# Where the gate products stand in a tile, and when the second group of scores is taken, in a fused attention and feed-forward kernel

## The chip, the cores and the metric

The kernel runs on one core of one Trainium2 chip. The metric is the device time of one launch in microseconds (us), lower is better. Engines: PE multiplies matrices, DVE, ACT and POOL work on tiles element by element, SP issues DMAs. Each engine takes its instructions in program order, and the order of the program is written out by hand.

## The reference

Linear attention with projected keys and values, then a gated feed-forward block on the result:

```python
k_proj = einsum('ks,bhsd->bhkd', E, k); v_proj = einsum('ks,bhsd->bhkd', F, v)   # B=H=8, S=1024, D=64, 64 rows
attn   = softmax(q @ k_proj^T / sqrt(D))                                          # over the 64 projected keys
x      = (attn @ v_proj) as [8192, 512]
g      = x @ w_gate                                                               # [8192, 1536]
out    = ((g * sigmoid(g)) * (x @ w_val)) @ w_out                                 # float32 [8192, 512]
```

## The kernel before, in words

The 8192 tokens are cut into 16 chunks `c` of 512 tokens, two to a batch `b`. The feed-forward block of a chunk runs in 12 tiles `f` of 128 gate columns, so there are 192 tiles, `t = 12c + f`. While the two chunks of batch b-1 run, the attention of batch b is worked in between them: `put(s, fn, ...)` puts a step into a slot, and tile t has slot 2t (between its gate and value products on PE) and slot 2t+1 (at its end). Slot numbers in `place(b)` count from the first tile of the even chunk of that stretch, so slot 23 is the end of tile 11 of the even chunk, and slot 25 the end of tile 0 of the odd one.

A tile runs in this order: `f_g` (gate matmuls, L536 into a `gps` bank, then Silu on ACT, L563), slot 2t, `f_v` (value matmuls, L536 into a `vps` bank), the list `late[t]`, slot 2t+1. There are two `gps` banks and two `vps` banks.

**Gate products.** A plain tile ends with one DVE product, L678: Silu of the gate times the value, read from its `vps` bank, written to `hT` in bf16. From chunk 4 on (in part from chunk 3) the tiles 2-3, 5-6 and 8-9 are paired: the value products of a pair are made with seven half-size products (L616) instead of eight, spread over three tiles. Tile p (2, 5 or 8) runs `p_34` in place of the value matmuls, and later in its `late` list `p_1`, which writes the other `vps` bank. Tile p+1 runs `p_52`, and tile p+2 (4, 7 or 10, itself plain) runs `p_76` before its value matmuls. `p_52` and `p_76` each end with a DVE sum L627, which empties the `vps` bank into `sx`, and a DVE product L634 of `thp` and `sx`, both in SBUF. `p_34` has the ACT copy L644, the Silu L646, which frees the `gps` bank of tile p, and the DVE sum L647.

**Output products.** The product with `w_out` of chunk c-1 runs during chunk c, also with seven half-size products, twice (for two halves of the tokens): `f_m(c, n)` takes them in the order 3, 4, 5, 2, 1, 6, 7. Products 1 and 6 stand together in `late` of tile 4 (first half) and tile 10 (second half), product 7 in tile 5 and tile 11. Called m1 to m7 here, each is 6 matmuls, L762. After m6 stands `m_16`: the DVE addition L791, which reads the bank that m1 wrote and that m7 will add to, and then the POOL subtraction L792. After m7 stands `m_7`: the DVE addition L797, which empties the bank and needs L792.

The operands of m1, m2, m5, m6 and m7 are sums of parts of `hT` (`h_sum`, L745). Those for m5 and m2 are made on POOL in tiles 7 to 11, one `f` at a time. Those for m1, m6 and m7 are made on DVE, each by one instruction, in tiles 1, 2 and 4 of the next chunk. The one for m7, here h7, is appended to `late` of tile 4 behind m1, m6 and L791, one tile ahead of m7. The operands that the paired tiles need of x are made by four DVE sums L607 (`p_x`), for an odd chunk all in tile 0.

**Attention steps.** `u_KV` projects keys and values, `u_KT` turns the keys and copies them into `BD` by two ACT and two DVE copies, one after another (L299 on DVE). `u_S` makes scores (L378) and takes Exp on ACT (L386), `u_R` sums and inverts on DVE (L408, L409), `u_N` normalises on POOL (L423, then a small L439), `u_AD` turns the result by a DMA that SP issues. A batch has eight `u_S`, j = 0 to 7, in two groups of four. Exp and Tanh share one function table of ACT, Silu is in another, and a change of table is an instruction of its own (ACT_TABLE_LOAD). So that the table changes twice for a group and not four times, the tile whose Silu falls between two pairs of scores is made with Tanh (the list `TANGENT`): Tanh on ACT, L560, and two DVE instructions, L681 and L684, in place of L678.

Of the kernel before, what the change touches and what calls it, by code (L numbers as in the profile page):

```python
# [10 lines left out]
ALU = mybir.AluOpType  # L11
# [4 lines left out]
B = 8  # L16
# [17 lines left out]
HT = CW // 2  # L34
ENG = [getattr(mybir.EngineType, n) for n in ("PE", "DVE", "Activation", "SP", "Pool")]
TANGENT = [(c, f) for c in range(CH) for f in range(NFT)] + [
    x for b in range(2, B) for x in ((2 * b - 2, 8 if b == 2 else 7), (2 * b - 1, 1))
]
PAIRED = {2: range(4, NC), 5: range(3, NC), 8: range(3, NC - 1)}
BY_DMA = [(b, ch) for b in range(1, B) for ch in range(CH)]  # L40
# [3 lines left out]
def kernel(  # L44
# [19 lines left out]
    nc = tc.nc  # L64
# [38 lines left out]
    kb, vb, qb, xT, hT = {}, {}, {}, {}, {}  # L103
# [421 lines left out]
    def f_mm(c, f, w, i=None):  # L525

        if i != 1:


            where = "y" if (c, f, w) == (0, 2, 0) else "gv"[w]  # L530
            half[c, f, w] = bank(where, [P, CW], FP32, where + "ps")
        ps = half[c, f, w]
        x = xT[divmod(c, CH)]
        ts = slice(0, CW) if i is None else slice(256 * i, 256 * (i + 1))
        for kt in range(NKT):
            nc.tensor.matmul(  # L536
                out=ps[:, ts],
                lhsT=(wg, wv)[w][:, kt, f * P : (f + 1) * P],
                rhs=x[:, kt, ts],
                start=(kt == 0),  # L540
                stop=(kt == NKT - 1),
            )
        return ps

    def paired(c, f):
        p = 3 * ((f + 1) // 3) - 1
        return p if not maxed and c in PAIRED.get(p, ()) and f < p + 2 else None

    def f_g(c, f, i=None):
        ps = f_mm(c, f, 0, i)  # L550
        p = paired(c, f)
        if p is not None:
            if f == p:
                gp["g"] = ps
            else:
                nc.scalar.activation(out=gp["p"][:, 1], in_=ps[:], func=AF.Silu)  # L556
            return
        th = fw.tile([P, CW], FP32, name="th", tag="th")
        if (c, f) in TANGENT and not maxed:
            nc.scalar.activation(out=th[:], in_=ps[:], func=AF.Tanh, scale=0.5)  # L560
            gp[0] = (ps, th)
        else:
            nc.scalar.activation(out=th[:], in_=ps[:], func=AF.Silu)  # L563
            gp[0] = (None, th)

    sums = {}

    def p_tiles():


        for n in range(2):
            a = q_pool.tile([P, 8, HT], BF16, name="xsa", tag=f"q0{n}", bufs=1)
            for m, x in ((6, a[:, 0:2]), (7, a[:, 2:4]), (67, a[:, 0:4]), (1, a[:, 4:6]), (3, a[:, 6:8])):
                sums["x", m, n] = x
        sums["x", 4, 0] = quarter(wo, 0, 1)[:, 4:6]
        sums["x", 4, 1] = x4[:]
        rows = [quarter(wo, 0, 1)[:, i] for i in range(4)] + [quarter(wo, 1, 0)[:, i] for i in range(HF)]
        for i, m in enumerate((1, 2, 5, 6, 7)):
            sums["w", m, 2] = wp[:, i]
            for n, f in enumerate((5, 8)):  # L580
                sums["w", m, f] = rows[5 * n + i].rearrange("p (k t) -> p k t", k=2)
# [47 lines left out]
    def p_h(c, p, part, v):  # L629
        h, th = (  # L630
            a.rearrange("p i t -> p (i t)").rearrange("p (i t) -> p i t", i=4)[:, part]
            for a in (hT[c][:, p : p + 2, :], gp["p"][:])
        )
        nc.vector.tensor_tensor(out=h, in0=th, in1=v, op=ALU.mult)  # L634

    def p_34(c, p):

# [16 lines left out]
    def p_52(c, p):  # L654
        x, sx = gp["x"], gp["sx"]
        p_mm(c, p, 5, x[:, 0])
        p_mm(c, p, 2, x[:, 1])
        p_sum(sx[:], gp["ts"][:, 0], x[:], ALU.subtract)
        p_h(c, p, slice(1, 3), sx[:])

    def p_76(c, p):
        x, sx = gp.pop("x"), gp.pop("sx")
        p_mm(c, p, 7, x[:, 0])
        p_mm(c, p, 6, x[:, 1])
        p_sum(sx[:], gp.pop("ts")[:, 1], x[:], ALU.add)
        p_h(c, p, slice(0, 4, 3), sx[:])
        gp.pop("p")

    def f_v(c, f, i=None):
        p = paired(c, f)  # L670
        if p is not None:
            return (p_34, p_52)[f - p](c, p)
        ps = f_mm(c, f, 1, i)
        g, th = gp.pop(0)
        if f == 0:
            hT[c] = h_pool.tile([P, NFT, CW], BF16, name="hT", tag="hT")
        if g is None:
            nc.vector.tensor_tensor(out=hT[c][:, f, :], in0=th[:], in1=ps[:], op=ALU.mult)  # L678
            return
        s1 = fw.tile([P, CW], FP32, name="s1", tag="s1", bufs=1)  # L680
        nc.vector.scalar_tensor_tensor(  # L681
            out=s1[:], in0=th[:], scalar=1.0, in1=g[:], op0=ALU.add, op1=ALU.mult
        )
        nc.vector.scalar_tensor_tensor(  # L684
            out=hT[c][:, f, :], in0=s1[:], scalar=0.5, in1=ps[:], op0=ALU.mult, op1=ALU.mult
        )
# [173 lines left out]
    def put(s, fn, *a):  # L860
        slots[s].append((fn, a))

    def place(b):
        s0 = 48 * (b - 1)
        if b == 1:
            put(22, u_TD, 1, 0)
            put(29, u_K1, 1)
            put(32, u_KT, 1)
            put(40, u_V1, 1)
            sa = (35, 36, 37, 38, 41, 42, 43, 44)  # L870
            put(41, u_AD, 1, 0)
            put(30, u_TD, 1, 1)
            put(47, u_AD, 1, 1)
            put(46, u_PVt, 1, 0, (0, 1), ("aa", "av"))
        else:
            if b == 2:
                put(s0 + 10, u_KV, b)
            else:
                put(s0 + 8, u_KV, b, "kv", (0, H), "v")
            put(s0 + (13 if b == 2 else 11), u_KT, b)  # L880
            put(s0 + (9 if b == 2 else -6), u_TD, b, 0)
            put(s0 + (11 if b == 2 else -4), u_TD, b, 1)
            sa = [s0 + j for j in ((15, 15, 17, 17) if b == 2 else (13, 13, 15, 15)) + (25, 25, 27, 27)]
            put(s0 + 29, u_AD, b, 0)
            put(s0 + 43, u_AD, b, 1)
            put(s0 + 44, u_PVt, b, 0, (0, 1), ("aa", "yz"))
        for j in range(NJ):
            put(sa[j], u_S, b, j)
            at = sa[j] + 1 if b == 1 else s0 + (
                17, 17 + 2 * (b == 2), 21 if b == 2 else 19, 23, 35, 37, 40, 41)[j]  # L890
            put(at, u_R, b, j)
            put(at, u_N, b, j)
        put(s0 + (68 if b == 1 else 56), u_PVt, b, 1, (0, 1), ("aa", "yz"))

    def run_slot(s):
        for fn, a in slots.pop(s, ()):
            fn(*a)
# [16 lines left out]
    def general():  # L914
# [6 lines left out]
        with tc.For_i(0, B) as turn, tc.manual_schedule():  # L921
            turn_of.append(turn)
            b = 0
            load_k(b)
            load_v(b)
            u_KV(b)
            u_KT(b)
            for ch in range(CH):
                c = CH * b + ch
                load_q(b, ch)  # L930
                for u in range(4 * ch, 4 * ch + 4):
                    u_T(b, u)
                    u_S(b, u)
                    u_R(b, u)
                    u_N(b, u)
                    u_A(b, u)
                u_PVt(b, ch, (0, 1), ("aa", "yz"))
                for f in range(NFT):
                    f_g(c, f)
                    f_v(c, f)  # L940
                for m in (1, 2, 5, 6, 7):
                    h_sum(c, m, 0, HF, nc.vector)
                for n in range(14):
                    f_m(c, n)

    with tc.manual_schedule():
# [3 lines left out]
        for i in range(2):  # L950
            nc.scalar.dma_start(
                out=kraw[i][:],
# [126 lines left out]
        for b in range(1, B):  # L1079
            place(b)  # L1080
        for b in range(2, B):
            s0 = 48 * (b - 1) - (20 if b == 3 else 24)
# [10 lines left out]
        late = defaultdict(list)  # L1093
# [25 lines left out]
        for c in range(3, NC):  # L1119
            for i, m in enumerate((4, 3, 1, 67)):  # L1120
                t = c * NFT + (0 if c % 2 else (-1, -1, 0, 0)[i])
# [7 lines left out]
        for t in range(NIT):  # L1129
            c, f = divmod(t, NFT)  # L1130
            ring["wide"] = c < 2
            i = 1 if t < 2 else None
            f_g(c, f, i)
            if "x" in gp and paired(c, f) is None:
                p_76(c, f - 2)
            run_slot(2 * t)
            f_v(c, f, i)
            for fn, *a in late.pop(t, ()):
                fn(*a)
            run_slot(2 * t + 1)  # L1140
        f_m_last(NC - 1)
# [33 lines left out]
```

## Time and profile before

| | us |
|---|---|
| median of 3 runs | 556.23 (556.15 to 557.1) |
| the profiled execution, its own time | 556.3 |
| its span, first to last instruction | 554.7 |
| PE busy | 532.3 (96%) |
| DVE busy | 436.0 (79%) |
| POOL busy | 343.9 (62%) |
| ACT busy | 293.5 (53%) |
| granted clock of PE | 1.000 |

From batch 3 on the trace repeats with a period of about 66.6 us, two chunks of 12 tiles. A row of the timeline holds the start, the time busy, the engine, the line, the operation, what is written and read with shapes, and in brackets how long the engine was idle ahead of it and which instruction ended that. The end of a matmul is modelled and lies some 0.16 us behind the time at which the next one can start, so the brackets of PE show that much too little; the time lost is read from the starts.

### The profile page before, as it was taken

How to read it: one execution, taken by the hardware profiler on the slowest of the kernel's cores; microseconds unless marked ns; L12 is line 12 of the kernel's file. 1: busy time of each engine (PE TensorE's matmuls, PEld its weight loads, DVE VectorE, ACT ScalarE, POOL GpSimd, SP SyncE). 2: the span in 40 equal slices, each digit the busy share in tenths (PEclk: the TensorE clock that was granted, in tenths of full speed). 3: DMA queues.
4: the chain of work that ended last, by engine and by line, in shares of the span. 5: the costliest groups of instructions: out<-in, count | busy, mean ns of one | idle time of the engine just before them, and what ended most of it. 6: DMA issues, size and time to landing. Idle time of an engine off the chain costs nothing. (4 is left out here: it accounts for less than half of the span.)

```text
span 554.7 us, 9971 instructions
## 1 busy us (share of the span) xinstructions
PE 532.3 (96%) x3712; PEld 334.4 (60%) x3780; DVE 436.0 (79%) x712; ACT 293.5 (53%) x527; POOL 343.9 (62%) x428
## 2 busy tenths in 40 slices
PE   7999999999999899999999999999999999999996
PEld 4654445566566565666666666565665666566665
DVE  3787885688878897789877887879887798875874
ACT  3564454674457644656546565565554844453431
POOL 7862494395925968178861878538683584835344
PEclk9999999999999999999999999999999999999999
DMA  9999969839901399105971179611993112200013
GB/s 199 191 197 189 176 143 181 161 78 193 224 1 39 86 201 207 40 2 122 209 163 39 41 113 212 132 39 40 155 204 99 39 52 63 77 37 16 26 40 116
DMA packets 112228, 62.94 MB, mean 113 GB/s; under 512 B 65968, under 2 KB 103856, under 8 KB 112176
## 3 DMA queue, kind: packets, MB, share of 16 engines
q0 software_dynamic: 43952, 29.49, 37.2%
q1 hardware_dynamic: 67392, 31.46, 22.6%
q10 hardware_dynamic: 832, 1.31, 0.8%
q8 instruction: 30, 0.49, 0.3%
q14 instruction: 22, 0.18, 0.1%
HBM read 60.29 MB, written 16.78 MB: 139 GB/s over the span
## 5 line engine op out<-in xcount | busy, mean ns | idle before, releaser
L536 PE MATMUL gps<-xT,wg 128*128 128x512 bf16 (+1 forms) x727 | 192.0, 377 | 5.0 <-ACT thp L646 3.3
L745 POOL TENSOR_TENSOR hs<-hT 128x256 bf16<-128x256 bf16 x180 | 133.7, 773 | 7.0 <-DVE hT L678 4.4
L536 PE MATMUL vps<-xT,wv 128*128 128x512 bf16 (+1 forms) x459 | 118.8, 376 | 1.4 <-DMA wv<-in_moe_w_val_dram 0.8
L536 PEld LDWEIGHTS <-wg 128*128 128x128 bf16 x776 | 74.0, 98 | 55.7 <-issue 4.7
L792 POOL TENSOR_TENSOR tt<-tt,ysb 128x512 f32<-128x512 f32 x28 | 43.7, 1560 | 101.0 <-DVE tt L791 98.9
L762 PEld LDWEIGHTS <-hs 128*128 128x128 bf16 x900 | 86.9, 98 | 31.6 <-issue 5.8
L563 ACT ACTIVATE th<-gps 128x512 f32<-128x512 f32 x82 | 49.0, 597 | 92.0 <-PE gps L536 87.2
L423 POOL TENSOR_TENSOR AAd<-ee,zr 128x512 bf16<-128x512 f32 x56 | 61.6, 1100 | 37.8 <-ACT ee L386 17.8
L536 PEld LDWEIGHTS <-wv 128*128 128x128 bf16 x480 | 45.1, 98 | 50.7 <-issue 6.5
L762 PE MATMUL yps<-ws,hs 128*128 128x256 bf16 x540 | 68.7, 273 | 6.0 <-DVE tt L791 3.8
L678 DVE TENSOR_TENSOR hT<-th,vps 128x512 bf16<-128x512 f32 x82 | 55.7, 679 | 23.0 <-PE vps L536 18.9
L634 DVE TENSOR_TENSOR hT<-thp,sx 128x512 bf16<-128x512 f32 x74 | 63.3, 856 | 6.4 <-ACT thp L556 1.8
L627 DVE TENSOR_TENSOR sx<-ts,vps 128x512 f32<-128x512 f32 x74 | 49.4, 667 | 12.2 <-PE vps L616 10.9
L781 POOL TENSOR_TENSOR tt<-xs 128x256 f32<-128x256 f32 x30 | 27.1, 905 | 46.5 <-ACT xs L779 46.5
L762 PE MATMUL yps<-ws,hT 128*128 128x256 bf16 x360 | 48.8, 273 | 0.6
L762 PE MATMUL yps<-wo,hs 128*128 128x256 bf16 x360 | 48.6, 273 | 0.1
L745 DVE TENSOR_TENSOR hs<-hT 128x1536 bf16<-128x1536 bf16 (+1 forms) x49 | 47.9, 985 | 0.0
L644 ACT COPY sx<-vps 128x512 f32<-128x512 f32 x37 | 21.7, 585 | 48.6 <-PE vps L616 48.0
L408 DVE TENSOR_REDUCE zr<-ee 128x8 f32<-128x512 f32 x64 | 42.9, 670 | 3.1 <-ACT ee L386 3.1
L762 PEld LDWEIGHTS <-hT 128*128 128x128 bf16 x360 | 35.2, 98 | 13.2
L386 ACT ACTIVATE ee<-sc 128x512 f32<-128x512 f32 x64 | 36.2, 602 | 9.6 <-POOL AAd L423 5.3
L647 DVE TENSOR_TENSOR ts<-sx 128x256 f32<-128x256 f32 x37 | 25.4, 688 | 16.8 <-ACT sx L644 16.8
(134 smaller groups left out, 741.5 us busy)
## 6 DMA issues: line engine op xcount, KB each, us to landing
out_dram<-ysb SPq DMA_DIRECT2D x27, 512.0 KB, 2.9
qb<-in_q_dram POOLq DMA_DIRECT2D x14, 512.0 KB, 18.0
kb<-in_k_dram POOLq DMA_DIRECT2D x7, 1024.0 KB, 10.4
vb<-in_v_dram POOLq DMA_DIRECT2D x7, 1024.0 KB, 16.6
wo<-in_moe_w_out_dram POOLq DMA_DIRECT2D x2, 768.0 KB, 21.7
out_dram<-ysb SPq DMA_DIRECT2D x6, 256.0 KB, 2.4
kraw<-in_k_dram ACTq DMA_DIRECT2D x2, 512.0 KB, 4.8
qb<-in_q_dram POOLq DMA_DIRECT2D x4, 256.0 KB, 7.9
```

The costliest lines, as they stand in the source:

```text
L386: nc.scalar.activation(out=e[:].rearrange("p h j k -> p (h j k)"), in_=ps[:].rearrange("p a k -> p (a k)"), func=AF.Exp, scale=scale,)
L408: nc.vector.reduce_sum(out=z, in_=e[:], axis=AX.X)
L423: eng.tensor_tensor(out=a.rearrange("p j h k -> p h j k"), in0=ee.pop((b, u))[:], in1=r.unsqueeze(3).to_broadcast([P, 4, 2, KP]), op=ALU.mult,
L536: nc.tensor.matmul(out=ps[:, ts], lhsT=(wg, wv)[w][:, kt, f * P : (f + 1) * P], rhs=x[:, kt, ts], start=(kt == 0), stop=(kt == NKT - 1),)
L563: nc.scalar.activation(out=th[:], in_=ps[:], func=AF.Silu)
L627: nc.vector.tensor_tensor(out=out, in0=a.unsqueeze(1).to_broadcast([P, 2, HT]), in1=b, op=op)
L634: nc.vector.tensor_tensor(out=h, in0=th, in1=v, op=ALU.mult)
L678: nc.vector.tensor_tensor(out=hT[c][:, f, :], in0=th[:], in1=ps[:], op=ALU.mult)
L745: eng.tensor_tensor(out=hs[c, m][:, fs, :], in0=quarter(hT[c], *a)[:, fs], in1=quarter(hT[c], *b)[:, fs], op=op,)
L762: nc.tensor.matmul(out=ps, lhsT=lhsT, rhs=ws[m][:, f, :] if rhs is None else rhs, start=(start and f == 0), stop=(f == HF - 1), skip_group ...
L781: nc.gpsimd.tensor_tensor(out=t[:, 0], in0=xs[:, 0], in1=xs[:, 1], op=ALU.add)
L792: nc.gpsimd.tensor_tensor(out=t[:], in0=t[:], in1=yo[c, p][:, 1:3], op=ALU.subtract)
```

## The change

Four things are changed together. Gate products L634 and L678 are no longer issued where they arise, but collected in a list `last` and issued by `gate()`. Up to chunk 2 that is at once. From chunk 3 on the list `late` of a tile is sorted: `f_m` and `p_1` first, with all that they issue on ACT, DVE, POOL and SP, then `gate()`, then the rest (`h_sum`, `p_x`). The Tanh tile's products L681 and L684 are not collected. The second group of scores moves two slots ahead (25, 25, 27, 27 to 23, 23, 25, 25), and with it the Tanh tile of the odd chunk, from tile 1 to tile 0. For batches from 3 on, `u_KT` moves one slot ahead (11 to 10, which is ahead of `p_34` in tile 5), and the sums and the normalising of j = 3 move from slot 23 to slot 21, the end of tile 10.

```diff
-    x for b in range(2, B) for x in ((2 * b - 2, 8 if b == 2 else 7), (2 * b - 1, 1))
+    x for b in range(2, B) for x in ((2 * b - 2, 8 if b == 2 else 7), (2 * b - 1, 0))
...
+    last = []
+
+    def gate():
+        for h, th, v in last:
+            nc.vector.tensor_tensor(out=h, in0=th, in1=v, op=ALU.mult)
+        last.clear()
...
-        nc.vector.tensor_tensor(out=h, in0=th, in1=v, op=ALU.mult)
+        last.append((h, th, v))
...
         if g is None:
-            nc.vector.tensor_tensor(out=hT[c][:, f, :], in0=th[:], in1=ps[:], op=ALU.mult)
+            last.append((hT[c][:, f, :], th[:], ps[:]))
+            if c < 3:
+                gate()
             return
...
-            put(s0 + (13 if b == 2 else 11), u_KT, b)
+            put(s0 + (13 if b == 2 else 10), u_KT, b)
...
-            sa = [s0 + j for j in ((15, 15, 17, 17) if b == 2 else (13, 13, 15, 15)) + (25, 25, 27, 27)]
+            sa = [s0 + j for j in ((15, 15, 17, 17) if b == 2 else (13, 13, 15, 15)) + (23, 23, 25, 25)]
...
-                17, 17 + 2 * (b == 2), 21 if b == 2 else 19, 23, 35, 37, 40, 41)[j]
+                17, 17 + 2 * (b == 2), 21 if b == 2 else 19, 23 if b == 2 else 21, 35, 37, 40, 41)[j]
...
-            for fn, *a in late.pop(t, ()):
+            todo = late.pop(t, [])
+            if c > 2:
+                todo.sort(key=lambda x: (x[0] not in (f_m, p_1)) * 2)
+                todo.insert(sum(x[0] in (f_m, p_1) for x in todo), (gate,))
+            for fn, *a in todo:
                 fn(*a)
```

## The prediction

> **What bounds the kernel now.** First the page's busy times: does any engine have room?
>
> ```profile
> PE 532.3 (96%) x3712; PEld 334.4 (60%) x3780; DVE 436.0 (79%) x712; ACT 293.5 (53%) x527; POOL 343.9 (62%) x428
> ```
>
> PE sets the time, and at its pace: four 128x512 matmuls take 0.86 us, six 128x256 ones 0.66. No matmul is added or taken away, so the change can only move PE's waits. Second, the waits of PE alone:
>
> ```profile
> PE yps L762 <- DVE tt L791: 3.8, 5, 1.0
> PE gps L536 <- ACT thp L646: 3.3, 5, 0.7
> PE yps L762 <- DVE hs L745: 2.0, 13, 0.2
> ```
>
> The first two come once per stretch of two chunks (five stretches, batches 3 to 7), the third 13 times: once per chunk from chunk 3 on. Third, the timeline where the first two arise:
>
> ```profile
> 446.32 0.68 DVE L678 TENSOR_TENSOR hT<-th,vps 128x512 bf16<-128x512 f32 x1
> 446.91 0.41 DVE L791 TENSOR_TENSOR tt<-tt,yps 128x256 f32<-128x256 f32 x1
> ...
> 447.38 0.82 PE L762 MATMUL yps<-ws,hs 128*128 128x256 bf16 x6 [0.71 <-DVE tt L791]
> ...
> 455.78 0.60 ACT L386 ACTIVATE ee<-sc 128x512 f32<-128x512 f32 x1 [1.06 <-POOL AAd L423]
> ...
> 456.88 1.28 ACT L646 ACT_TABLE_LOAD   x1
> ...
> 458.82 1.02 PE L536 MATMUL gps<-xT,wg 128*128 128x512 bf16 x3 [0.66 <-ACT thp L646]
> ```
>
> m7 of an even chunk's tile 11 waits for L791, which stands behind two gate products. The odd chunk's tile 4 waits for a `gps` bank that L646 frees late, behind the last Exp (held up by POOL) and a table load. Last, tile 4 of an odd chunk, where the third wait arises:
>
> ```profile
> 460.98 1.47 PE L762 MATMUL yps<-ws,hs 128*128 128x256 bf16 x12
> 461.08 0.69 DVE L634 TENSOR_TENSOR hT<-thp,sx 128x512 bf16<-128x512 f32 x1
> 461.69 0.68 DVE L678 TENSOR_TENSOR hT<-th,vps 128x512 bf16<-128x512 f32 x1
> ...
> 462.56 0.42 DVE L791 TENSOR_TENSOR tt<-tt,yps 128x256 f32<-128x256 f32 x1 [0.19 <-PE yps L762]
> 462.89 0.95 DVE L745 TENSOR_TENSOR hs<-hT 128x1536 bf16<-128x1536 bf16 x1
> ...
> 463.12 1.85 POOL L792 TENSOR_TENSOR tt<-tt,ysb 128x512 f32<-128x512 f32 x1 [5.79 <-DVE tt L791]
> ```
>
> DVE does both gate products while PE still runs m1 and m6, then idles 0.19 until m6 ends. L791, h7 (L745) and m7 follow in a chain, and PE already waits at its end: it could start m7 at 462.29 + 0.86 + 0.44 = 463.59 and does at 463.90, 0.31 lost. Tile 4 of an even chunk is alike: L791 at 428.83, h7 at 429.17, m7 at 430.17 for 429.86.
>
> **What goes, for a stretch.** m7 in even tile 11 could start at 445.63 + 0.87 = 446.50, not 447.38: 0.88. The gate matmuls of odd tile 4 wait 0.66 + 0.16 (hidden in the modelled end) = 0.82. The start of `p_52` one tile before, 456.91 for 455.88 + 0.86 behind L644: 0.17. In even tile 6 the scores stop for the last copy into `BD` (L299 to 433.44; scores begin at 433.13, go on at 433.50): 0.31. All together 2.18, over five stretches 10.9.
>
> **What comes in tile 4.** The sort puts m1, m6 and L791 first, then the gate products, then h7. L791 can't run sooner, it waited for PE before as well; so DVE idles until m6 ends, and L634 and L678 are then done inside the chain. From starts in the rows above: L634 holds DVE 0.61 (461.08 to 461.69), L678 about 0.60 (446.32 to 446.91 for the same step). That makes h7 1.21 later, and none is hidden, since PE waits there already. The nearest row for h7 itself is where DVE reached an L745 while POOL was adding:
>
> ```profile
> 418.81 1.45 DVE L745 TENSOR_TENSOR hs<-hT 128x1536 bf16<-128x1536 bf16 x1
> ...
> 419.40 1.44 POOL L781 TENSOR_TENSOR tt<-xs 128x256 f32<-128x256 f32 x1
> ```
>
> 1.45 beside 0.95. Another, at 455.53 beside the end of an L423, took 1.04. In before h7 began ahead of L792; now L792 starts some 0.6 after m6's end, h7 some 1.6 after, and L792 takes 1.26 to 1.85: it is under way. I add 0.40, between 0.09 and 0.50 and nearer the upper row, as L792 lasts longest. Per chunk 1.21 + 0.40 = 1.6 (1.21 to 1.71). Twelve chunks (4 to 15) pay it: 19.2. Chunk 3 has no L634 in tile 4: 0.60 + 0.40 = 1.0 (0.6 to 1.1).
>
> The Trainium skill ("SBUF — State Buffer", Who interferes with whom) says of a DVE instruction with two SBUF inputs beside a GpSimd one that reads SBUF that the second to issue blocks fully. By it L792 waits for L634 and h7 for all of L792, which by the trace's durations ends m7's wait about 1.85 later per chunk; the sum below would be 3 to 4 us more, near 575. The 1.45 fits, but no row shows this order of three.
>
> **What comes around the second group.** In the times above, m6 of even tile 10 ends at 444.94, DVE is free of L627 at 445.2, L791 ends at 445.65, m7 runs from 446.50 to 447.16. The first scores follow to 447.61 (0.45 by 450.41 to 450.86), table load 0.47 after their start at 447.63, Tanh 2.26 after that (450.88 to 453.14) at 449.89, done at 450.49. Then L681 and L684 (1.47, 454.14 to 455.61) to 451.96, the four L607 (3.37, 450.77 to 454.14) to 455.25, and only then L678 of tile 1 to 455.9. `p_1` of tile 2 writes the bank which that product reads. PE comes to it at 447.61 + 2.83 (tile 0: 0.86 + 0.86 + 0.66 + 0.45 for scores) + 2.38 (tile 1: 0.86 + 0.86 + 0.66) + 1.96 (tile 2: 0.86 + 0.44 + 0.66) = 454.78: a new wait of 1.17. In before Tanh stood in tile 1, behind the L607, and its L684 ended at 455.61, when PE arrived at 455.66. From 455.95 on: `p_1` 0.22, tile 3 1.96, so tile 4 at 458.13 for 458.82; DVE's queue (two L745, L647, L627) then holds `p_76` about 0.1. So of 0.88 + 0.17 + 0.82 = 1.87 there remain 0.58, between 0 and 1.87: 2.9 over five (0 to 9.35). I take the worked value, since each term is a distance that the trace shows for the same steps; the bounds are `p_1` waiting for nothing and taking all.
>
> The Trainium skill ("ScalarE: Activation LUTs", What ACT_TABLE_LOAD costs) gives 1.28 for a load and about 1.38 for a drain. The load agrees, the drain isn't seen: Exp starts at 452.17, the load ended at 452.16. With a drain `p_1` would wait 1.38 more, and the sum be 7 higher; the row decides.
>
> **What moves at no cost, and its cover.** `u_KT`: its ACT copies now stand ahead of L644 and its DVE copies ahead of L647. In even tile 5, h7 ends near 431.7, the copies near 433.0, L644 near 433.15, and PE comes to `p_52` at about 433.5; scores at 434.6. So the 0.31 goes (1.55 in five); with the 0.35 of cover gone, it would cost the rest. POOL: normalising j = 3 (L423, L439, up to 1.7) passes six L745 of tile 11. Exp no longer waits for it; the last sum for m5 ends near 454.5 for 454.1, inside the wait of `p_1`, else 0.4 a stretch. SP: the transposing DMA, issued at 455.78 when L423 ends, can go some 5 us sooner; nobody waits. Banks: L678 of even tile 10 is done near 447.2, that of tile 11, now behind L797, near 449.4; their banks are wanted at 448.5 and 450.4 + 0.9 = 451.3, and a cover gone would cost PE the excess in each stretch. L634 and L678 of odd tile 10 end near 413.25, the bank is wanted at 414.55.
>
> **The sum.** 19.2 + 1.0 - 1.55 - 2.9 = +15.75 on the profiled execution's 556.3 (span 554.7, and 1.6 around it, which stays; the median, 556.23, is the same within 0.1): 572.0.
>
> **Rivals.** *The gain whole, the cost bare*: `p_1` waits for nothing (Tanh or the L607 quicker) and h7 isn't slowed: 12 x 1.21 + 0.6 - 10.9 = +4.2, 560.5. For it: POOL is done with L792 sooner if nothing meets it; against: 1.45 above. *The gain lost*: `p_1` eats all of it and h7 takes the 0.50: 12 x 1.71 + 1.1 - 1.55 = +20.1, 576.4. *Faster*: tile 4's products run beside PE after all, so h7 is no later, and all four waits go: 545.4. It decides at a price of 10.9/13 = 0.84 per chunk in tile 4 with the gain whole, 0.34 with my gain; two products at 0.6 are above both, and the one tile without L634 is chunk 3's. Against it: L791 waited for PE in tile 4 and in odd tile 10 before, so putting it ahead frees nothing there; it does only in even tile 10. *The change not doing what it says*, no wait gone and tile 4 paying: 556.3 + 12 x 1.6 + 1.0 = 576.5, inside the range.
>
> **How the numbers follow.** Forecast with its bounds 0.68; gain whole, cost bare 0.14; gain lost or worse 0.12; a price near break-even 0.02, half of it within 0.2% and half faster; all four waits gone at no price 0.04. The range runs from 560.5 to 577 (576.4 rounded up). Slower by over 0.2% (1.1 us, about what a measurement of this kernel can tell) 0.94, within 0.01, faster 0.05.
>
> **What would show it.** Right: PE's wait for L745 at over 1 us in 13 places, DVE idle over 1 us ahead of L791 in tile 4, PE's waits for L791, L646 and in `BD` gone, a new one of L616 for L678 once a stretch. The period of two chunks is then 66.6 + 2 x 1.6 - 0.31 - 0.58 = 68.9. Wrong: m7 in tile 5 no later, or h7 ahead of L634 on DVE; a period under 66.6 would overturn it.

## The result, and the profile after

The changed kernel takes 576.2 us (median of 6 runs, 575.75 to 576.73) against 556.29 for the one before: 1.0356 times as long, interval 1.0343 to 1.037. The profiled execution took 575.75 us with a span of 574.2. The forecast was 572.0, range 560.5 to 577.

Lines have new numbers in the changed file. Products with the gate are now all L571 (L634 and L678 before); L745 is L753, L762 is L770, L791, L792 and L797 are L799, L800 and L805; L607, L616 and L627 are L613, L622 and L633; L644, L646 and L647 are L650, L652 and L653; L681 and L684 are L689 and L692.

The waits of PE, in the changed kernel:

```profile
PE yps L770 <- DVE hs L753: 22.9, 13, 1.9
PE vps L622 <- DVE hT L571: 6.6, 5, 1.4
```

The waits for L791 and L646 that headed the list before are gone. The wait for h7, 2.0 us in 13 places before, is 22.9 in the same 13 places, and a new one, of `p_1` for the product of tile 1, stands once in each of the five stretches. Tile 4 of an odd chunk, changed kernel, with start, time busy and engine first as before:

```profile
475.83 0.82 PE L770 MATMUL yps<-ws,hs 128*128 128x256 bf16 x6
...
476.75 0.42 DVE L799 TENSOR_TENSOR tt<-tt,yps 128x256 f32<-128x256 f32 x1 [1.55 <-PE yps L770]
477.09 0.69 DVE L571 TENSOR_TENSOR hT<-thp,sx 128x512 bf16<-128x512 f32 x1
...
477.32 1.58 POOL L800 TENSOR_TENSOR tt<-tt,ysb 128x512 f32<-128x512 f32 x1 [7.68 <-DVE tt L799]
...
477.69 0.68 DVE L571 TENSOR_TENSOR hT<-th,vps 128x512 bf16<-128x512 f32 x1
...
478.29 1.43 DVE L753 TENSOR_TENSOR hs<-hT 128x1536 bf16<-128x1536 bf16 x1
...
479.77 0.39 PE L770 MATMUL yps<-ws,hs 128*128 128x256 bf16 x2 [1.83 <-DVE hs L753]
```

DVE now idles 1.55 us for m6 where it idled 0.19, with both products queued behind L799. L799 itself begins no sooner after m6 than it did. The products run after it, h7 after them, and m7 starts at 479.77 for 477.78 (gate matmuls from 476.48, 0.86, `p_34`, 0.44): 1.99 lost where 0.31 was. And h7 takes 1.43 in place of 0.95: it is issued while POOL's subtraction runs, and ends 0.82 after that does (478.90 to 479.72).

Tiles 0 to 2 of an odd chunk, the rows of DVE alone and then the first of PE's:

```profile
465.06 0.69 DVE L689 SCALAR_TENSOR_TENSOR s<-th,gps 128x512 f32<-128x512 f32 x1 [1.53 <-ACT th L560]
465.85 0.69 DVE L692 SCALAR_TENSOR_TENSOR hT<-s,vps 128x512 bf16<-128x512 f32 x1
466.45 0.99 DVE L613 TENSOR_TENSOR x<-xT 128x512 bf16<-128x512 bf16 x1
467.37 2.83 DVE L613 TENSOR_TENSOR xsa<-xT 128x512 bf16<-128x512 bf16 x3
470.12 0.67 DVE L571 TENSOR_TENSOR hT<-th,vps 128x512 bf16<-128x512 f32 x1
```

```profile
470.84 0.38 PE L622 MATMUL vps<-xsa,wp 128*128 128x256 bf16 x2 [1.40 <-DVE hT L571]
```

DVE stands idle 1.53 us for Tanh, does the Tanh tile's two instructions and the four sums of x, and only then the product that empties the bank of `p_1`. PE was there 1.40 + 0.17 = 1.57 us before (1.17 in the first of the five stretches, 1.56 in the others).

### The profile page after: what moved, and what is told of

It is laid out like the page before. It is cut to its first block, busy times and chain, and to the rows that moved or that the text cites. A ratio compares the mean times of both kernels' runs of the same rounds, so it can differ in the third digit from the quotient of the medians.

```text
span 574.2 us, 10005 instructions
## 1 busy us (share of the span) xinstructions
PE 534.8 (93%) x3780; PEld 334.2 (58%) x3780; DVE 435.3 (76%) x712; ACT 294.5 (51%) x527; POOL 329.4 (57%) x428
## 4 chain that ended last, share of the span: by engine, by line
PE 80%; DVE 12%; POOL 3%; DMA 2%; issue 1%; ACT 1%; DVEq 0%; ACTq 0%; POOLq 0%
PE gps L536 25%; PE yps L770 21%; PE vps L536 16%; PE vps L622 9%; DVE hT L571 3%; DVE hs L753 3%; DVE xsa L613 2%; DMA wv<-in_moe_w_val_dram 2%; PE sc L378 2%; PE kvp L187 2%; PE yps L704 2%; PE pv L482 1%; DVE tt L799 1%; ACT ee L386 1%; POOL hs L753 1%
## 5 line engine op out<-in xcount | busy, mean ns | idle before, releaser
L536 PE MATMUL gps<-xT,wg 128*128 128x512 bf16 (+1 forms) x772 | 196.5, 377 | 0.5
L753 POOL TENSOR_TENSOR hs<-hT 128x256 bf16<-128x256 bf16 x180 | 132.6, 766 | 7.1 <-DVE hT L571 4.4
L536 PE MATMUL vps<-xT,wv 128*128 128x512 bf16 (+1 forms) x480 | 121.7, 376 | 0.9 <-DMA wv<-in_moe_w_val_dram 0.8
L770 PEld LDWEIGHTS <-hs 128*128 128x128 bf16 x900 | 87.0, 98 | 48.0 <-DVE hs L753 26.5
L800 POOL TENSOR_TENSOR tt<-tt,ysb 128x512 f32<-128x512 f32 x28 | 42.1, 1503 | 112.0 <-DVE tt L799 112.0
L770 PE MATMUL yps<-ws,hs 128*128 128x256 bf16 x540 | 68.7, 273 | 23.0 <-DVE hs L753 22.9
L423 POOL TENSOR_TENSOR AAd<-ee,zr 128x512 bf16<-128x512 f32 x56 | 58.5, 1044 | 47.5 <-ACT ee L386 17.8
L571 DVE TENSOR_TENSOR hT<-thp,sx 128x512 bf16<-128x512 f32 x74 | 64.1, 866 | 4.1
L571 DVE TENSOR_TENSOR hT<-th,vps 128x512 bf16<-128x512 f32 x82 | 55.6, 678 | 8.6 <-PE vps L536 5.3
L633 DVE TENSOR_TENSOR sx<-ts,vps 128x512 f32<-128x512 f32 x74 | 49.9, 674 | 12.0 <-PE vps L622 10.3
L789 POOL TENSOR_TENSOR tt<-xs 128x256 f32<-128x256 f32 x30 | 22.9, 763 | 59.8 <-ACT xs L787 59.7
L753 DVE TENSOR_TENSOR hs<-hT 128x1536 bf16<-128x1536 bf16 (+1 forms) x49 | 56.7, 1163 | 0.1
L770 PE MATMUL yps<-ws,hT 128*128 128x256 bf16 x360 | 48.8, 273 | 0.0
L770 PE MATMUL yps<-wo,hs 128*128 128x256 bf16 x360 | 48.6, 272 | 0.1
L770 PEld LDWEIGHTS <-hT 128*128 128x128 bf16 x360 | 35.2, 98 | 13.3
L650 ACT COPY sx<-vps 128x512 f32<-128x512 f32 x37 | 21.7, 586 | 38.3 <-PE vps L622 35.9
L689 DVE SCALAR_TENSOR_TENSOR s<-th,gps 128x512 f32<-128x512 f32 x35 | 23.6, 675 | 18.5 <-ACT th L560 17.7
```

The costliest lines, as they stand in the source:

```text
L423: eng.tensor_tensor(out=a.rearrange("p j h k -> p h j k"), in0=ee.pop((b, u))[:], in1=r.unsqueeze(3).to_broadcast([P, 4, 2, KP]), op=ALU.mult,
L536: nc.tensor.matmul(out=ps[:, ts], lhsT=(wg, wv)[w][:, kt, f * P : (f + 1) * P], rhs=x[:, kt, ts], start=(kt == 0), stop=(kt == NKT - 1),)
L633: nc.vector.tensor_tensor(out=out, in0=a.unsqueeze(1).to_broadcast([P, 2, HT]), in1=b, op=op)
L689: nc.vector.scalar_tensor_tensor(out=s1[:], in0=th[:], scalar=1.0, in1=g[:], op0=ALU.add, op1=ALU.mult)
L753: eng.tensor_tensor(out=hs[c, m][:, fs, :], in0=quarter(hT[c], *a)[:, fs], in1=quarter(hT[c], *b)[:, fs], op=op,)
L770: nc.tensor.matmul(out=ps, lhsT=lhsT, rhs=ws[m][:, f, :] if rhs is None else rhs, start=(start and f == 0), stop=(f == HF - 1), skip_group ...
```

## The experiments

Theory: the loss is made in tile 4, where products stand in the chain from m6 to m7, and at `p_1`; only even tile 10 and the earlier scores gain. The rivals are a DVE that is late as a whole, so that waits would only change places, and two parts that cost only together. All runs are compared with the kernel before on the same chip.

| kernel | us | ratio to before | interval |
|---|---|---|---|
| the change | 576.2 | 1.0356 | 1.0343 to 1.037 |
| t4_before | 554.80 | 0.9972 | 0.9961 to 0.9983 |
| px67_later | 573.59 | 1.0307 | 1.029 to 1.0324 |
| no_sub | 570.75 | 1.0256 | 1.0239 to 1.0273 |
| sched_only | 555.25 | 0.9981 | 0.9971 to 0.9991 |
| gate_only | 574.50 | 1.0323 | 1.0306 to 1.034 |
| t10_sched | 552.74 | 0.9933 | 0.9917 to 0.995 |
| t10_alone | 551.44 | 0.9911 | 0.9894 to 0.9927 |
| t10_sched_px | 545.86 | 0.9809 | 0.9793 to 0.9825 |
| t4_one | 572.73 | 1.0296 | 1.0281 to 1.0312 |
| t10_sched_px_h7 | 542.49 | 0.975 | 0.9736 to 0.9763 |

**t4_before.** The products of tile 4 go back to where they arise.

```diff
                 p_76(c, f - 2)
+                if f == 4:
+                    gate()
...
-            if c < 3:
+            if c < 3 or f == 4:
                 gate()
```

> The changed kernel with the two gate products of tile 4 alone put back to where they arise, ahead of m1, m6 and L791; all else as changed. Theory (tile 4's chain costs): the 13 waits of PE for h7, together 20.9 us above the 0.32 each that they cost before, go back to 0.32: 576.2 - 20.9 = 555.3 (554 to 557), the wait of p_1 in tile 2 of odd chunks stays near 1.5. Rival (the time is lost elsewhere, and m7 only shows it: the DVE as a whole is late): the wait moves to another place of the same chunk and less than half comes back, over 566.

554.8: 21.4 us came back by moving 25 instructions. PE's list is led by the wait of `p_1`, unchanged, and h7 is back at its old size:

```profile
PE vps L622 <- DVE hT L571: 6.6, 5, 1.4
...
PE yps L770 <- DVE hs L753: 1.2, 8, 0.2
```

Nothing moved elsewhere, so DVE isn't late as a whole. In the five even chunks where `u_KT` now stands ahead of `p_34` the wait for h7 is smaller, 0.20 for 0.32 from start to start, and too small for the list (8 places for 13).

**no_sub.** Is h7 slow because of POOL?

```diff
+        if p or c < 3:
-        nc.gpsimd.tensor_tensor(out=t[:], in0=t[:], in1=yo[c, p][:, 1:3], op=ALU.subtract)
+            nc.gpsimd.tensor_tensor(out=t[:], in0=t[:], in1=yo[c, p][:, 1:3], op=ALU.subtract)
```

> The changed kernel without the POOL subtraction L792 in tile 4 of chunks 4 to 15; half of the rows of the output lack that term. Theory (shared access to SBUF: h7 waits for POOL's subtraction to end): h7 takes 0.95 and not 1.43, so each of the 12 waits of m7 shrinks by 0.48: 5.8 us, 570.4, and the price of two gate products is then 1.2 a chunk. Rival (h7 is slow for a reason of DVE's own, or the price is the sum of the instructions put ahead of it): h7 stays at 1.4, the time within 1 us of 576.2.

570.75, 5.45 us less than the change. Tile 4 of an odd chunk in this kernel:

```profile
405.70 0.42 DVE L799 TENSOR_TENSOR tt<-tt,yps 128x256 f32<-128x256 f32 x1 [1.34 <-PE yps L770]
...
406.09 0.69 DVE L571 TENSOR_TENSOR hT<-thp,sx 128x512 bf16<-128x512 f32 x1
...
406.70 0.68 DVE L571 TENSOR_TENSOR hT<-th,vps 128x512 bf16<-128x512 f32 x1
...
407.30 0.95 DVE L753 TENSOR_TENSOR hs<-hT 128x1536 bf16<-128x1536 bf16 x1
```

h7 takes 0.95 again, with the same instructions ahead of it. What is left, 1.1 to 1.2 a chunk, is the two products themselves.

**t4_one.** The kernel before, with only the plain product of tile 4 held back. `gate()` and the sorting of `late` are as in the change, the schedule is as it was before. The numbers of lines behind the products (L571) are one higher here than in the changed kernel: L800 is the addition, L801 POOL's subtraction, L754 h7, L771 the output products.

```diff
         last.append((h, th, v))
+        gate()
...
-            if c < 3:
+            if c < 3 or f != 4:
                 gate()
```

> The kernel before, with one product alone held back: the plain one of tile 4, from chunk 3 on, behind L791 and ahead of h7. Theory (h7 waits for POOL's subtraction to end, whatever stands ahead of it): h7 is reached 1.05 us after m6's end, L792 runs from 0.67 to 1.93, h7 ends 0.82 after that, and each of 13 chunks loses 1.35: 556.4 + 17.6 = 574 (573 to 575). Rival (the price is the length of the instructions put ahead, 0.6 for one): 556.4 + 13 x 0.6 = 564.2.

572.73, so one product costs 16.3 us where the length of the instructions would give 7.8. The waits for h7 lie 17.7 above those of before (13 places at 1.68 for 0.32). Tile 4 of an odd chunk:

```profile
405.69 0.42 DVE L800 TENSOR_TENSOR tt<-tt,yps 128x256 f32<-128x256 f32 x1 [0.79 <-PE yps L771]
...
406.03 0.68 DVE L571 TENSOR_TENSOR hT<-th,vps 128x512 bf16<-128x512 f32 x1
...
406.26 1.26 POOL L801 TENSOR_TENSOR tt<-tt,ysb 128x512 f32<-128x512 f32 x1 [2.15 <-DVE tt L800]
...
406.63 1.71 DVE L754 TENSOR_TENSOR hs<-hT 128x1536 bf16<-128x1536 bf16 x1
```

POOL's subtraction reads SBUF alone and so does h7: h7, reached at 406.63, ends at 408.34, 0.82 after POOL's 407.52. The product held back here reads its value from PSUM, and POOL was not delayed by it (1.26). The first product of the changed kernel reads SBUF twice, and there POOL took 1.58. So the price isn't a sum of instructions: one product costs 1.36 a chunk since it lets POOL go first, the second only 0.3 more. The 1.4 us between the waits and the time lie in even tile 6: PE comes there later by the longer wait for h7, and the 0.31 that it lost to `BD` in each of the five stretches is gone, 1.5 in all (the eight score matmuls run from 445.50 without a gap). The theory had left that out, so 572.73 is just under its 573 to 575.

**sched_only and gate_only.** The two halves of the change, each alone. sched_only calls `gate()` at every `last.append` and leaves `late` unsorted; gate_only has the slots and the Tanh tile of before:

```diff
-    ... (2 * b - 1, 0))
+    ... (2 * b - 1, 1))
...
-            put(s0 + (13 if b == 2 else 10), u_KT, b)
+            put(s0 + (13 if b == 2 else 11), u_KT, b)
...
-            sa = ... + (23, 23, 25, 25)]
+            sa = ... + (25, 25, 27, 27)]
...
-                17, 17 + 2 * (b == 2), 21 if b == 2 else 19, 23 if b == 2 else 21, 35, 37, 40, 41)[j]
+                17, 17 + 2 * (b == 2), 21 if b == 2 else 19, 23, 35, 37, 40, 41)[j]
```

> The kernel before with only the moved schedule (second group of scores, Tanh tile, u_KT, sums and normalising of j = 3) and the gate products where they were. Theory (the waits for the gps bank, L644 and BD go, 1.30 a stretch, but Tanh in tile 0 puts tile 1's product behind the four sums of x and p_1 waits 1.2 to 1.6 for it; the 0.88 for L791 stays): -6.5 + 6 to 8, 557 (556 to 558.5). Rival (the schedule's gain comes whole, p_1's wait comes from the deferral of products): 556.3 - 6.5 = 549.8.

> The change's first part alone: gate products behind f_m and p_1 in every tile from chunk 3 on, with the schedule of before. Theory (each part pays where the waits say): 556.4 + 20.9 for h7 in tile 4, - 4.6 for L791 in even tile 10, + 2.1 for the products of tile 7 that now stand behind the Tanh tile's two and hold L644 of tile 8 (0.43 five times); the 0.82 for the gps bank stays: 574.8 (573 to 577). Rival (the loss comes from both parts meeting, each alone is small): under 565.

555.25 and 574.5. The schedule alone gains 1.2 us, where I expected a loss of half a us: `p_1` waits in it without any deferral, so that wait comes from the Tanh tile's move, but 1.04 and not 1.2 to 1.6. The difference to the 1.57 of the change lies in the sums of x, which take 3.14 here (385.13 to 388.27) and 3.67 there; POOL's sums run beside the first of them in both, which takes 0.52 here and 0.99 there. The deferral alone costs 18.1 us, nearly as much as the change with its 19.9, so the loss doesn't need both parts. Added up, the halves make 16.9. Of the 3.0 that they lack, 1.5 is the wait for `BD`, which goes in each of them and can go only once; the rest wasn't split. In gate_only the wait for the `gps` bank didn't stay at 0.82 as I expected. In its place stand 0.48 of `p_1` for the Tanh tile's product, 0.35 for the bank and 0.30 of `p_76`, so that its time fell on the forecast is in part luck.

**px67_later.** The longest sum of x goes behind tile 1's product.

```diff
-                late[t].append((p_x, c, m))
+                late[t + (c % 2 and m == 67)].append((p_x, c, m))
```

> The changed kernel with the longest of the four sums of x of an odd chunk (L607 of before, 1.1 to 1.2 us, an operand of p_76 only) moved from tile 0 to the end of tile 1, behind tile 1's gate product. Theory A (the order on DVE is what p_1 pays for): p_1's wait falls from 1.57 to 0.4 and 5 x 1.15 = 5.8 us come back, 570.4. Theory B (DVE as a whole is the limit from tile 0 to tile 4 of the odd chunk, since it did not start before Tanh was done): the wait moves on to p_76 in tile 4, whose bank L627 frees with only some 0.4 us to spare, and only about 5 x 0.4 = 2 to 2.5 us come back, 573.8. The rest of the change is as before: no other wait moves.

573.59: theory B. The wait of `p_1` fell, and one of `p_76` for its bank (L633) came:

```profile
PE vps L622 <- DVE sx L633: 2.9, 4, 1.1
...
PE vps L622 <- DVE hT L571: 1.0, 4, 0.3
```

Reordering inside tiles 0 to 4 of an odd chunk gives back 2.6 of the 5.8 us; DVE there has too much to do after Tanh.

**t10_sched and t10_alone.** Products are held back in tile 10 alone, with the new and with the old schedule (the latter as in gate_only).

```diff
         last.append((h, th, v))
+        if p < 8 or part.step is None:
+            gate()
...
-            if c < 3:
+            if c < 3 or f != 10:
                 gate()
```

> The whole change, but products are held back in tile 10 alone; in all other tiles they stand where they arise. Theory: as with tile 4 put back (554.8), less the 0.26 + 0.17 that even tile 10 lost five times: 552.6 (552 to 553.5), and p_1 still waits 1.5 in tile 2 of odd chunks. Rival (the small waits of tile 10 come from the scores' earlier place, not from tile 7's products): 554.8.

> The schedule of before, and products held back in tile 10 alone. Theory (the only place where L791 stood behind products while PE waited for it): 556.4 - 5 x 0.88 and a little = 551.8 (551.3 to 552.5). Rival (what m7 gains there is lost again behind the last Exp and the table load, since POOL and ACT are late anyway): 555 to 556.

552.74 and 551.44. The second is the change's one good idea by itself: 4.9 us for the 0.88 at five places (1.16 at the first, 4.7 in all). The first, beside t4_before, shows where another 2.1 us went. In the changed kernel, even tiles 7 and 8:

```profile
451.72 0.69 DVE L692 SCALAR_TENSOR_TENSOR hT<-s,vps 128x512 bf16<-128x512 f32 x1
...
452.32 0.69 DVE L571 TENSOR_TENSOR hT<-thp,sx 128x512 bf16<-128x512 f32 x1
...
453.10 0.59 ACT L650 COPY sx<-vps 128x512 f32<-128x512 f32 x1 [0.45 <-DVE hT L571]
...
453.70 1.28 ACT L652 ACT_TABLE_LOAD   x1
...
455.65 1.02 PE L536 MATMUL gps<-xT,wg 128*128 128x512 bf16 x4
```

The paired product of tile 7 stands behind the Tanh tile's two, which aren't collected. The ACT copy writes `sx` which that product reads, so it waits to 453.10, the table load and the Silu follow it, and tile 10's gate matmuls start 0.26 late, its `p_76` 0.17.

**t10_sched_px.** t10_sched, with two of the four sums of x of an odd chunk made in tiles 6 and 7 of the even one.

```diff
+                if c % 2 and c > 3 and m in (1, 67):
+                    t -= NFT - (7 if m == 1 else 6)
                 late[t].append((p_x, c, m))
```

> As t10_sched, and two of the four sums of x of an odd chunk (from chunk 5 on) moved from tile 0 to tiles 6 and 7 of the even chunk before, where DVE idles. Theory (p_1 waits because DVE starts those sums only after Tanh): with 2 us less on DVE between Tanh and tile 1's product p_1's wait of 1.57 goes in all five stretches: 552.6 - 7.8 = 544.8 (544 to 546.5). Rival (DVE is short of time in tiles 6 to 9 as well and the waits come back there): over 549.

545.86, 6.9 us less than t10_sched, where the five waits of `p_1` come to 7.4 (1.17 in the first stretch) and not 7.8, and the wait of `p_1` is off PE's list. So moving the Tanh tile pays once DVE has the room.

**t10_sched_px_h7.** And h7 one tile sooner.

```diff
-                        late[(c + 1) * NFT + 4].append((h_sum, c, 7, 0, HF, nc.vector))
+                        late[(c + 1) * NFT + (3 if c > 1 else 4)].append((h_sum, c, 7, 0, HF, nc.vector))
```

> As t10_sched_px, and h7 one tile sooner, at the end of tile 3 from chunk 3 on. Theory (what PE still waits for in tile 5 of odd chunks is the chain m6, L791, h7): 8 waits of 0.32 go, 545.9 - 2.6 = 543.3 (542.8 to 544.5). Rival (DVE in tiles 1 to 4 of the odd chunk has no room for 0.95 us more ahead of L627 of tile 4, and another wait takes the place): 545.5 to 547.

542.49: 2.5% less than before, the fastest of all, and 0.3 under the range that I had given. The waits of 0.20 in the five even chunks, which I hadn't counted, went too: 1.0 us beside the 2.6. Its busy times on the page:

```profile
PE 528.6 (98%) x3713; PEld 335.3 (62%) x3780; DVE 423.8 (78%) x712; ACT 293.5 (54%) x527; POOL 330.5 (61%) x428
```

From batch 3 on no wait of PE is over 0.4 us in its trace.

## Why the prediction was right

**Tile 4.** Forecast 12 x 1.6 + 1.0 = 20.2; the 13 waits grew by 20.9 (1.55 in the five even chunks with `u_KT`, 1.67 in most others, 1.36 in chunk 3). The products' 1.21 was right (no_sub), and so was the sign of POOL's share, but its size was drawn between two rows, and the first was read beside the wrong POOL instruction. These stood beside them in the profile before:

```profile
417.70 1.75 POOL L745 TENSOR_TENSOR hs<-hT 128x256 bf16<-128x256 bf16 x2
...
454.71 1.04 POOL L423 TENSOR_TENSOR AAd<-ee,zr 128x512 bf16<-128x512 f32 x1
...
455.53 1.04 DVE L745 TENSOR_TENSOR hs<-hT 128x1536 bf16<-128x1536 bf16 x1
```

DVE's sum of 418.81 ended at 420.26, 0.81 after POOL's 419.45; the L781 that the prediction shows beside it started later and was itself held. The sum of 455.53 ended 0.82 after POOL's 455.75. That is the 0.82 of the changed kernel and of t4_one, so the size could have been worked out: L634 done 1.29 after m6 (0.60 to its start, 0.69 long), L792 1.13 after that (as it ended 1.13 after h7 in the kernel before), h7 0.82 after that, together 3.24 for 1.55: 1.69 later, measured 1.67. The 0.82 is the same whether DVE reached its sum 0.22, 0.61 or 0.89 before POOL was done, which speaks for a block and against a mere slowing.

What the Trainium skill says ("SBUF — State Buffer", Who interferes with whom), that the second to issue blocks fully, agrees with these runs: POOL held by the product (1.58 for 1.26), h7 held by POOL (1.43, and 1.71 in t4_one). The 1.85 a chunk that the prediction worked out by that page was too high by 0.2, as it put the instructions end to end by their full durations; that its sum, near 575, came close is luck, since the 0.2 stands in for losses elsewhere. Chunk 3 is where the drawn value failed most, 1.0 for 1.36.

**Around the second group.** The chain was right step by step: scores, load 0.48 after, Tanh 2.27 after that, done 465.02, the Tanh tile's two 1.48. The mis-sized term is the four sums of x: 3.37 forecast, 3.67 measured (466.45 to 470.12). In the kernel before, in the changed one and in sched_only, POOL's own sums run beside them, and the first of the four ends some 0.28 after one of POOL's:

```profile
450.57 0.67 POOL L745 TENSOR_TENSOR hs<-hT 128x256 bf16<-128x256 bf16 x1
450.77 0.76 DVE L607 TENSOR_TENSOR x<-xT 128x512 bf16<-128x512 bf16 x1
```

```profile
466.48 0.68 POOL L753 TENSOR_TENSOR hs<-hT 128x256 bf16<-128x256 bf16 x1
```

```profile
384.70 0.67 POOL L753 TENSOR_TENSOR hs<-hT 128x256 bf16<-128x256 bf16 x1
385.13 0.52 DVE L613 TENSOR_TENSOR x<-xT 128x512 bf16<-128x512 bf16 x1
```

The first two rows are of the kernel before, the third stands beside the changed kernel's 466.45, the last two are of sched_only. So the first sum takes 0.76, 0.99 or 0.52 by where DVE meets POOL's row of sums, and a duration taken over from another place in the trace doesn't hold here: it makes 0.23 of the 0.30 that were missing. In the changed kernel POOL's sum of 466.48 went ahead of DVE's, whose row starts at 466.45 while an earlier POOL sum still ran; the starts of rows alone don't tell which goes first. With the last product `p_1` waited 1.57 for the 1.17 forecast (1.17 in the first stretch): 1.6 us over five stretches.

**What I called free.** That the ACT copy of tile 8 waits for tile 7's paired product, and that this product falls behind L681 and L684, I had left out: 0.43 a stretch, 2.15 us; t4_before less t10_sched is 2.1. The moves that I did name (`u_KT`, the normalising of j = 3, the banks of tiles 10 and 11) cost PE nothing that its list of waits shows.

**The gains.** 0.88, 0.82, 0.17 and 0.31 went, as forecast; sched_only shows that the schedule alone takes away the 0.82 and the 0.31, t10_alone that the 0.88 is tile 10's. The 0.31 goes in t4_one and gate_only too, where m7 is late, so a late m7 is enough for it.

The sum again with the waits of both traces, read from start to start and added up over the five stretches: +20.9 for h7, +7.4 for `p_1`, +2.1 for tile 7's product, +0.5 for `p_76` of odd tile 4, -9.6 for the 0.88, 0.82 and 0.17 (the first stretch had lost 1.16 to L791 and not 0.88), -1.5 for `BD`: +19.8, where the two profiled executions are 575.75 - 556.3 = 19.45 apart. The forecast was +15.75. Of the 4.05 between, tile 4 is 0.7, `p_1` 1.55 and tile 7 2.1, while the gains were larger by 0.3. The period of two chunks went from 66.6 to 69.6, for 68.9 forecast.

So the direction, the place of the loss and its size in tile 4 were foreseen, but not the rest: of the 2.9 that I expected to keep around the second group nothing was left. The time lies nearer to the rival "the gain lost", 576.4, which I gave 0.12, than to the forecast of 572.0.

The rival "faster" named its point, 0.84 a chunk in tile 4. The price without POOL's share, 1.2, was over it already.

## What to carry to other kernels

An addition that frees a bank gains from going first only where other work on its own queue is what holds it. Where it waits for another engine, work put behind it is work moved out of the cover into the chain. Ask for each place by itself: of the 26 tiles 4 and 10 in which the order changed around L791, five gained 0.87 or more, 13 lost 1.4 to 1.7, and the other eight neither. And an instruction whose operand release others wait for (here the copy into `sx`) counts as a reader with a deadline, even when its own result isn't urgent.

## What the runs showed of the hardware that I had not expected

The price of work put into a chain wasn't additive: one product of 0.68 us cost 1.36 a chunk, two cost 1.67. What sets it is whether h7 or POOL's subtraction, which both read SBUF alone, comes first; the record of the other then grows (h7 0.95 to 1.43 and 1.71; POOL's subtraction 1.26 to 1.85 behind h7 in the kernel before, and to 1.58 behind the first product) and no idle time is shown. In these traces a long record of h7 beside a POOL instruction that ends some 0.8 us before it is a wait, not slow work.
